# A fused linear-attention and gated-MLP kernel: decays by row transfers, and other orders, banks and holds

## The chip, the cores and the metric

The kernel runs on one core of one Trainium2 chip. The metric is device time in microseconds (us) of one execution; lower is better. The kernel before took 194.99 us, the median of three runs (193.37 to 195.72). The profile was taken in one further execution of 193.01 us, of which 191.3 us are the span from the first to the last instruction.

## What is computed

Attention with a decaying state over 4 batches, 8 heads, 768 steps, head size 48; then a gated feed-forward net (FFN) over the 3072 tokens, 384 wide, 1536 hidden:

```python
f = 1.0 / (1.0 + np.exp(-f_logit))
for t in range(S):
    state = f[:, :, t, :, None] * state + np.einsum('bhd,bhe->bhde', k[:, :, t], v[:, :, t])
    y[:, :, t] = np.einsum('bhd,bhde->bhe', q[:, :, t], state)
...
gate = np.maximum(x @ w_gate, 0.0)
val = x @ w_val
return (gate * val @ w_out).astype(np.float32)
```

## The kernel before, in words

Time is cut into six chunks of 128 steps. A *position* w = 4c + b (c from 0 to 5, b from 0 to 3) is one chunk of one batch; two positions make a *unit*. The first four units (positions 0 to 7, UNITS = 4) hold two chunks of one batch each, read as 96-float rows in which even and odd steps lie side by side; from position 8 on, a position is chunk c of batch b.

For each position the *front* (function `front`) turns f into negative log decays on ScalarE (ACT): `ef` (line 484, Exp) and `ln` (line 487). TensorE (PE) sums them over time with a triangular matrix: `cum` (lines 505 and 509 for the first units, 514 and 517 after). Line 517 makes four 1-column matmuls more, the sums over the whole chunk. ACT then forms `ek` (line 528, the growing factor) and `eq` (line 530, the shrinking one) in the tile `expo`, and from the whole-chunk sums the chunk's decay `dc` (line 538 for the first units, 545 after). `hk` and `hq` (lines 552 on GpSimd, called POOL, and 553 on VectorE, called DVE) multiply k and q by them into `hats`. The hats are turned by PE and copied back for positions 0 to 7 (`tk`, `tq`, line 564; copies `ck`, `cq`, lines 568 and 569), and by a DMA transpose from position 8 on (`xh`, line 572). `v` (lines 582 to 584) is a copy of v in bf16.

The scores `s` (lines 596, 662) are masked by DVE (`m`, lines 604, 669) into `ptm`. `y` (757, 764, 768, 684) and `yi` (720) give the chunk's output, `kv` (784, 707) what the chunk adds to the state, and `st` (454), or `ss` and `sd` (458, 460), the new state, scaled by the chunk's decay. The output becomes `x` (line 609), the FFN's turned input `xT`.

The FFN takes four positions at a time: `g` and `u` (line 804, the gate and value projections, 12 column groups of 128 each), `r` (relu, lines 809 and 810), `p` (line 812, the product), `o` (line 825), `d` (the copy out, 831 and 832), `S` (the store, 835). For chunk 0 the first four groups are done in halves: g00.0 to g00.3 for positions 0 and 1, g02.0 to g02.3 for positions 2 and 3 (256 columns instead of 512).

Loads are `L` with f, k, q or v, the chunk and the first position, so Lk0.2 (k0.2 in short) loads k for positions 2 and 3, the second unit; a load is 384 KB. They are issued from SyncE's queue (SP) and from ACT's. Weights come in column slices from POOL's queue, wg0+2 being groups 0 and 1 of w_gate.

Every operation is declared once with its reads, writes and possible engines (the class `Plan`). The order on each engine is then written out by hand of a planner, as lists of operation numbers (`ORDER`, line 24), and so are the PSUM banks in the order in which PE opens them (`BANKS`). From these the program works out which semaphore each instruction waits on. In PE's list `~3512` stands for three filler matmuls of 512 columns on zeros, put ahead of the next operation. `HELD` makes one operation wait for another that it doesn't need: in the kernel before, Lq0.0 for a memset, wv2+2 for hk02, Lq1.0 for yi03, Lv1.2 for tq13, wv8+4 for g02.1, wo0+4 for r00.6.

## Time and profile before

| what | value |
|---|---|
| median of three runs | 194.99 us |
| profiled execution, its time | 193.01 us |
| its span | 191.3 us |
| instructions in it | 4793 |
| granted TensorE clock | 1.0 throughout |
| moved by DMA | 32.43 MB |
| DMA packets under 512 B | 103472 of 110278 |

In the lines of the profile, `L804` is line 804 of the kernel; `ps<-xT,wg` names the tile written and the tiles read; `x219` is a count; a duration is in microseconds where a start stands before it, and in nanoseconds where it is a mean. What stands in brackets, or behind a bar with an arrow, is the idle time of the engine just before, and what ended it. PE's ends are modelled, so neighbouring matmuls overlap in the list; start to start is exact. PEld is PE's loading of weights.

### The profile page before, as it was taken

Reading aid. Unit: us, or ns where it says so; the run is one execution under the profiler, and the core shown is the slowest. Engines: PE = TensorE matmul, PEld = TensorE weight load, DVE = VectorE, ACT = ScalarE, POOL = GpSimd, SP = SyncE. Lnnn points to the kernel's source line nnn. Section 1 sums busy time; section 2 is a strip of 40 time slices with the busy share of each in tenths; the row PEclk is TensorE's granted clock in tenths of the full one; section 3 lists DMA queues with packets and bytes.
Section 4 is the critical chain, followed back from the end, with each engine's and each line's share of the span. In section 5 each row is a group of like instructions: output and inputs, shape, how many; then the busy total and the mean of one; then the engine's idle time right before and its main releaser. Section 6 shows DMA issues by size and latency. Waiting matters only on the chain.

```text
span 191.3 us, 4793 instructions
## 1 busy us (share of the span) xinstructions
PE 180.6 (94%) x1977; PEld 108.4 (57%) x1996; DVE 137.4 (72%) x249; ACT 92.0 (48%) x200; POOL 59.2 (31%) x88
## 2 busy tenths in 40 slices
PE   7597999989899999999999999999999999999994
PEld 7364785455655556655555654556656554455562
DVE  4299877986758778669868779988688485655620
ACT  3969663264477546497654574372233132301112
POOL 5638531741036702047371610492600000000000
PEclk9999999999999999999999999999999999999999
DMA  6999999969999999989999999999763300000223
GB/s 163 318 296 216 159 209 264 161 123 251 225 221 206 240 201 246 235 191 200 197 182 215 245 175 175 243 251 178 98 151 108 99 4 0 3 0 0 109 98 126
DMA packets 110278, 32.43 MB, mean 170 GB/s; under 512 B 103472, under 2 KB 110000, under 8 KB 110256
## 3 DMA queue, kind: packets, MB, share of 16 engines
q1 hardware_dynamic: 88960, 25.04, 61.7%
q0 software_dynamic: 3744, 3.54, 12.2%
q10 hardware_dynamic: 17552, 3.54, 10.0%
q8 instruction: 16, 0.26, 0.6%
q14 instruction: 6, 0.05, 0.1%
HBM read 25.95 MB, written 4.72 MB: 160 GB/s over the span
## 4 chain that ended last, share of the span: by engine, by line
PE 85%; DVE 8%; DMA 3%; issue 2%; ACT 0%; DVEq 0%; ACTq 0%
PE ps L804 46%; PE ps L825 25%; DVE hats L553 4%; DMA q_in<-in_q_dram 3%; PE ps L596 2%; PE ps L757 2%; PE ps L564 2%; PE ps L514 1%; DVE gT L812 1%; PE ps L662 1%; PE ps L684 1%; PE ps L784 1%; DVE ptm L669 1%; PE ps L768 1%; PE ps L764 1%
## 5 line engine op out<-in xcount | busy, mean ns | idle before, releaser
L812 DVE TENSOR_TENSOR gT<-relu,ps 128x512 bf16<-128x512 bf16 (+1 forms) x76 | 47.7, 653 | 19.7 <-PE ps L804 17.5
L804 PE MATMUL ps<-xT,wv 128*128 128x512 bf16 (+1 forms) x220 | 53.6, 367 | 0.6 <-issue 0.2
L804 PE MATMUL ps<-xT,wg 128*128 128x512 bf16 (+1 forms) x219 | 52.6, 368 | 0.6
L825 PE MATMUL ps<-wo,gT 128*128 128x384 bf16 (+2 forms) x300 | 52.0, 320 | 0.0
L809 ACT ACTIVATE relu<-ps 128x512 bf16<-128x512 f32 (+1 forms) x42 | 23.9, 576 | 47.8 <-PE ps L804 24.2
L825 PEld LDWEIGHTS ps<-wo,gT 128*128 128x128 bf16 x300 | 27.7, 98 | 18.3
L804 PEld LDWEIGHTS ps<-xT,wg 128*128 128x128 bf16 x228 | 23.6, 108 | 20.5 <-issue 0.4
L804 PEld LDWEIGHTS ps<-xT,wv 128*128 128x128 bf16 x228 | 23.3, 108 | 18.3
L552 POOL TENSOR_TENSOR hats<-q_in,expo 128x384 bf16<-128x384 f32 x17 | 17.9, 1058 | 30.2 <-DMA q_in<-in_q_dram 12.2
L810 DVE TENSOR_SCALAR relu<-ps 128x512 bf16<-128x512 f32 (+1 forms) x34 | 21.7, 654 | 5.4 <-PE ps L804 5.3
L552 POOL TENSOR_TENSOR hats<-k_in,expo 128x384 bf16<-128x384 f32 x17 | 17.7, 1050 | 21.2 <-ACT expo L528 14.9
L604 DVE TENSOR_TENSOR ptm<-ps,tri 128x512 bf16<-128x512 f32 x32 | 20.5, 684 | 5.1 <-PE ps L596 5.1
L831 ACT ACTIVATE osb<-ps 128x384 f32<-128x384 f32 (+1 forms) x16 | 7.6, 484 | 25.0 <-PE ps L825 22.2
L528 ACT ACTIVATE expo<-ps 128x384 f32<-128x384 f32 x24 | 11.7, 496 | 6.1 <-DVE hats L553 2.6
L530 ACT ACTIVATE expo<-ps 128x384 f32<-128x384 f32 x24 | 11.8, 492 | 2.0 <-PE ps L517 1.9
L460 POOL TENSOR_TENSOR st<-ssum,dec 128x384 bf16<-128x384 f32 x10 | 8.6, 864 | 10.0 <-DVE ssum L458 10.0
L669 DVE TENSOR_TENSOR ptm<-ps,tmask 128x512 bf16<-128x512 f32 x16 | 10.0, 678 | 2.1 <-PE ps L662 2.1
L484 ACT ACTIVATE f_in<-f_in 128x768 f32<-128x768 f32 x12 | 10.1, 840 | 2.8 <-DMA f_in<-in_f_logit_dram 2.8
L458 DVE TENSOR_TENSOR ssum<-ps,st 128x384 f32<-128x384 f32 x16 | 8.8, 550 | 2.7 <-PE ps L784 2.5
L553 DVE TENSOR_TENSOR hats<-q_in,expo 128x384 bf16<-128x384 f32 x7 | 8.2, 1167 | 3.4 <-DMA q_in<-in_q_dram 3.4
L487 ACT ACTIVATE bneg<-f_in 128x768 bf16<-128x768 f32 x12 | 10.1, 841 | 1.0 <-ACT osb L831 0.8
L564 PE MATMUL ps<-ident,hats 128*128 128x128 bf16 x64 | 5.5, 220 | 4.0 <-DVE hats L553 3.0
(78 smaller groups left out, 159.2 us busy)
## 6 DMA issues: line engine op xcount, KB each, us to landing
v_in<-in_v_dram SPq DMA_DIRECT2D x12, 384.0 KB, 5.5
out_dram<-osb SPq DMA_DIRECT2D x23, 192.0 KB, 2.3
k_in<-in_k_dram SPq DMA_DIRECT2D x10, 384.0 KB, 7.1
q_in<-in_q_dram SPq DMA_DIRECT2D x9, 384.0 KB, 5.8
f_in<-in_f_logit_dram SPq DMA_DIRECT2D x8, 384.0 KB, 4.8
f_in<-in_f_logit_dram ACTq DMA_DIRECT2D x4, 384.0 KB, 6.6
q_in<-in_q_dram ACTq DMA_DIRECT2D x3, 384.0 KB, 5.6
wv<-in_moe_w_val_dram POOLq DMA_DIRECT2D x2, 384.0 KB, 6.7
```

The costliest lines, as they stand in the source:

```text
L484: add(f"ef{c}{b0}", by("ACT", lambda: sc.activation(raw, raw, AF.Exp, scale=-1.0), act_(n)), keys, keys, key=P)
L528: add(f"ek{c}{b}", by("ACT", lambda: sc.activation(ex[:, 1, :], bc.ap[:, 0:HD], AF.Exp, scale=1.0), act_(HD)), [bc], [f"expk{ei}"], key=P + 1)
L530: add(f"eq{c}{b}", by("ACT", lambda: sc.activation(ex[:, 0, :], bc.ap[:, 0:HD], AF.Exp, scale=-1.0), act_(HD)), [bc], [f"expq{ei}"], key=P ...
L552: return {**by("POOL", lambda: gp.tensor_tensor(o, i_, e_, ALU.mult), pool_(HD)), **by("DVE", lambda: ve.tensor_tensor(o, i_, e_, ALU.mult ...
L553: **by("DVE", lambda: ve.tensor_tensor(o, i_, e_, ALU.mult), dve_(HD))}
L604: add(f"m{c}{b}{j}", by("DVE", lambda b=b, j=j, mi=mi: ve.tensor_tensor(ptm[mi][:, j, :, :], s[b, j].ap[:, :].rearrange("p (n t) -> p n t" ...
L669: add(f"m{c}{b2[i]}{j}", by("DVE", lambda i=i, j=j, mask=mask: ve.tensor_tensor(ptm[mi[i]][:, j, :, :], s[j, i].ap[:, :].rearrange("p (n t ...
L804: z = te.matmul(bank.ap[:, 0:n], wt[:, kt, w_cols(j)], xT[xi][:, kt, n0:n1], start=(kt == 0), stop=(kt == NK - 1))
L809: add(f"r{c}{b0}.{j}", {**by("ACT", lambda: sc.activation(rdst, gate.ap[:, 0:n], AF.Relu), act_(n)), **by("DVE", lambda: ve.tensor_scalar_ ...
L810: **by("DVE", lambda: ve.tensor_scalar_max(rdst, gate.ap[:, 0:n], 0.0), dve_(n))}, [gate], [f"relu{ri}"], key=P)
L812: add(f"p{c}{b0}.{j}", by("DVE", lambda: ve.tensor_tensor(gT[gi][:, j, n0:n1], rdst, val.ap[:, 0:n], ALU.mult), dve_(n)), [val, f"relu{ri} ...
L825: z = te.matmul(o.ap[:, 0:e1 - e0], gT[gi][:, j, b * C:(b + 1) * C], wo[:, j, e0:e1], start=(j == 0), stop=(j == NJ - 1))
```

## The change

*Decays by rows.* For positions 8 to 19 the sums of line 517 and the exponentials of line 545 are left out. The decay of a whole chunk is the last row of `eq`, so it is taken from there: partition 127 of `expq` is spread over 48 partitions of the tile `dec`, by two small DMAs for each pair of positions (`xd`; six steps of two DMAs, each of 48 pieces of 32 bytes). So that eight floats that belong together lie side by side, `eq` writes its result with a step of 64 bytes in these positions, and `hq` reads it so. `dec` changes its layout to match.

*Buffers.* `expo` becomes `expk` with 2 buffers and `expq` with 4 (2 pairs), in place of 3 of both. `zeros` shrinks from 512 to 128 columns (wide fillers read it repeatedly); `tlow` is laid over a sum buffer. `FOLD` (4) stands where `UNITS` (4) stood in `place`, and loads from position 8 on go through `place`.

*Orders, banks and holds.* All five lists and all banks are new. The opening filler is 12 matmuls of 512 columns, not 60 of 100. SP begins f0.0, q0.0, f0.2, k0.0, f1.0, k0.2, q0.2, f1.2, k1.0, v0.0, v0.2, q1.2, k1.2, q1.0, v1.2, f2.2 (before: f0.0, f0.2, k0.0, v0.0, k0.2, v0.2, q0.2, f1.2, f1.0, q1.2, q1.0, k1.0, k1.2, v1.2, v1.0, f2.0, with q0.0 on ACT). POOL takes wv2+2 first of all weights. PE's list up to the first FFN matmul, g00.0, now holds the cums of positions 4 to 7 too. Holds: Lv0.2 for eq03, S11 for eq42, Lv2.0 for hk21.

```diff
-NB, NE, NH, NQ, NM, NV, NA, NN, NS, NX, NG, NR, NO = 3, 3, 6, 6, 5, 6, 3, 4, 2, 2, 2, 4, 3
+NB, NE, NH, NQ, NM, NV, NA, NN, NS, NX, NG, NR, NO = 3, 2, 6, 6, 5, 6, 3, 4, 2, 2, 2, 4, 3
+FOLD = 4
+ROW_DECAYS = set(range(8, 20))
+NEQ = 2
...
-        45, ~60100, 74, 85, ~3512, 82, ~3512, 90, 80, 92, 121, ~1512, 95, 110, 101, 126, ~4512, 116, ~2512, 100, 128,
+        45, ~12512, 74, 85, ~6512, 110, ~1512, 80, 121, ~2512, 92, 82, 90, ~3512, 230, 95, 118, 116, ~2512, 128,
...
-    48: 10, 57: 114, 60: 140, 67: 284, 69: 164, 70: 185,
+    55: 123, 357: 694, 371: 389,
...
-    expo = sb("expo", [128, NE, 2, HD], F32)
+    expk, expq = sb("expk", [128, NE, HD], F32), sb("expq", [128, NEQ, 2, HD], F32)
...
-    decs = sb("dec", [128, NA, B, NP, 2], F32)
+    decs = sb("dec", [128, NA, 2, B, NP], F32)
...
-            if c < NC - 1:
+            if ch < NC - 1 and not rows:
                 for p in range(NP):
                     x = te.matmul(bc.ap[:, HD + p:HD + p + 1], bn[:, 2 * p:2 * p + 2, :].rearrange("p h d -> p (h d)"), ones[:, :])
...
+        ex = (expq[:, eqi, :, :].rearrange("q x h -> q (x h)").rearrange("q (d j x p) -> q x p j d", d=D, x=2, j=2)[:, b % 2, :, :, :] if rows
+              else expq[:, eqi, b % 2, :].rearrange("q (p j d) -> q p j d", p=NP, j=2),
+              expk[:, ei, :].rearrange("q (p j d) -> q p j d", p=NP, j=2))
...
+            def decay_rows(eng):
+                for j in range(2):
+                    at, to = expq[C - 1:C, eqi, 0, 2 * NP * j:2 * NP * j + 1], decs[64 * j:64 * j + D, ai, j, b0, 0:1]
+                    x = eng.dma_start(bass.AP(tensor=to.tensor, offset=to.offset, ap=[list(to.ap[0]), [1, 2 * NP]]),
+                                      bass.AP(tensor=at.tensor, offset=at.offset, ap=[list(at.ap[0]), [4 * NP, D], [1, 2 * NP]]))
+                    if j == 0:
+                        x.then_inc(xd.sem, 16)
+                return x
...
```

## The prediction

> **What bounds the kernel now.** I read the page first, then busy time by stage, then the chain of work in order of time, then the start instruction by instruction.

> ```profile
> PE 180.6 (94%) x1977; PEld 108.4 (57%) x1996; DVE 137.4 (72%) x249; ACT 92.0 (48%) x200; POOL 59.2 (31%) x88
> PE 85%; DVE 8%; DMA 3%; issue 2%; ACT 0%; DVEq 0%; ACTq 0%
> ```

> The tensor engine is busy for 94% of the span and makes 85% of the chain that ends last. A gain must therefore be PE work that goes, a shorter start, or a gap closed in the middle. Busy time by stage says where such gaps are (columns: stretch, length, then PE, PEld, DVE, ACT and POOL, each with its instructions, the granted clock, the DMA share, GB/s):

> ```profile
> 0.00:19.84 19.84, 14.55 (x300) 10.70 (x303) 13.39 (x42) 14.41 (x27) 11.49 (x34) 1.00 1.01 243
> 19.84:35.00 15.16, 14.99 (x190) 10.17 (x183) 12.34 (x24) 7.56 (x20) 5.84 (x8) 1.00 1.15 210
> 35.00:55.00 20.00, 18.40 (x348) 11.46 (x349) 16.26 (x28) 9.54 (x19) 5.78 (x9) 1.00 1.07 197
> 55.00:120.00 65.00, 64.68 (x658) 36.89 (x662) 49.86 (x85) 41.41 (x98) 25.27 (x27) 1.00 1.12 209
> 120.00:180.00 60.00, 59.38 (x436) 33.65 (x443) 42.75 (x68) 17.16 (x35) 10.85 (x13) 1.00 0.44 92
> 180.00:191.30 11.30, 8.61 (x63) 5.51 (x61) 2.83 (x5) 1.87 (x5) 0.00 (x0) 1.00 0.35 127
> ```

> Length less PE's busy time gives its idle time: 5.29 us before 19.84 (and part of its busy time there is filler on zeros), 1.60 us between 35 and 55, 0.94 us in the 125 us after that, 2.69 us at the end. From 55 to 180 us there is next to nothing to win by order, only something to lose. The start and the stretch from 35 to 55 decide.

> ```profile
> 4.16 0.84 ACT L484 ACTIVATE f_in<-f_in 128x768 f32<-128x768 f32 x1 [2.07 <-DMA f_in<-in_f_logit_dram]
> 7.10 0.87 ACT L528 ACTIVATE expo<-ps 128x384 f32<-128x384 f32 x2
> 8.06 0.99 POOL L552 TENSOR_TENSOR hats<-k_in,expo 128x384 bf16<-128x384 f32 x1 [1.38 <-ACT expo L528]
> 8.19 1.28 DVE L553 TENSOR_TENSOR hats<-q_in,expo 128x384 bf16<-128x384 f32 x1 [3.35 <-DMA q_in<-in_q_dram]
> 10.30 0.55 DVE L553 TENSOR_TENSOR hats<-q_in,expo 128x384 bf16<-128x384 f32 x1
> 17.14 0.60 ACT L609 ACTIVATE xT<-ps 128x384 bf16<-128x384 f32 x1
> 19.13 0.59 DVE L609 CAST xT<-ps 128x384 bf16<-128x384 f32 x1
> 19.84 0.50 PE L804 MATMUL ps<-xT,wg 128*128 128x256 bf16 x3
> ```

> The first FFN matmul starts at 19.84, when DVE has written the second xT block (x01, 19.13 to 19.72). The start hangs on DVE: it began hq00 at 8.19, when the q load had landed, and needed 11.53 us from there to the end of x01, almost without a gap.

> **The change, part by part.** *Decays by rows.* For positions w = 8 to 19 the four 1-column matmuls behind each cum go, and two small ACT exponentials with them; six steps of two small DMAs each come instead.

> ```profile
> 55.66 0.16 PE ps L514
> 55.82 0.08 PE ps L517 x4
> 55.90 2.61 PE ps L804 x12
> 61.47 0.70 ACT L545 ACTIVATE dec<-ps 64x4 f32<-64x4 f32 x4
> 71.51 0.83 POOL L460 TENSOR_TENSOR st<-ssum,dec 128x384 bf16<-128x384 f32 x1 [5.73 <-DVE ssum L458]
> L413 ACTq DMA_DIRECT2D f_in<-in_f_logit_dram x4: 374/374/1402, 46.8 to 75.6; - x4
> qkT<-hats SPq DMA_TRANSPOSE x16, 3.3
> DMA to landing us min/median/max: 2.7/3.3/8.2
> ```

> On a full PE the four cost 0.08 us (55.82 to 55.90). There are 12 such groups, all in PE's full stretch: 12 x 0.08 = **-0.96**. ACT loses 24 exponentials of 0.175 us (four in 0.70), 4.2 us, and gets the 12 DMA issues, since all six xd stand on its list. No row has so small a transfer there; a full load costs 0.37 us to issue and 1.40 at worst, so 4.4 to 16.8 us in all, and I take 4.4, because the median of that row is its minimum. ACT is free for 23.6 of the 65 us after 55, which hides either end; without that cover the surplus (0.2 to 12.6) would delay relus and so PE. The landing is bounded by the nearest transfers between SBUF tiles, the transposes of hats: 2.7 to 8.2 us, median 3.3 (the last two rows). A state update that needs a decay of chunk 2 ran at 71.51 and had been waiting for DVE's sum, ten microseconds after that chunk's last decays (61.47). So even 8.2 us is hidden, and I take 0; with the slack gone, the update on POOL would hold up the hats queued behind it, and these the next scores.

> *Strided expq.* In these positions eq writes, and hq reads, one float in every 64 bytes. No row shows such a step. The nearest are ACT's copy to x00 with a 4-byte step, 0.60 us, and a plain ek, 0.44: from 0 to +0.5 us for each of 12 eq and 12 hq, and I take the middle. That is 3 us on ACT and up to 3 on POOL, which is busy for 25.3 of the 65 us after 55: hidden, 0 on the path.

> *Expk from 3 buffers to 2, expq to 4.* An ek now waits for the hk two positions back instead of three. The price lies between 0 (ACT is 48% busy) and one hat on POOL, 1.05 us by a row below, for each time that it bites; I take 0, since in the new lists each hk stands shortly behind its ek. *Zeros, tlow, the layout of dec, FOLD*: shorter memsets and the same values (FOLD equals UNITS, so place and load do what they did): 0.

> *The new start.* SP now issues f0.0, q0.0 (from ACT's list, 0.37 us less there), f0.2, k0.0, f1.0, k0.2, q0.2, f1.2, k1.0, v0.0, and holds v0.2 until eq03; v1.0 moves to ACT (0.37 more), behind a relu; wv2+2 goes first on POOL, with no hold.

> ```profile
> GB/s 0 0 77 188 326 324 320 297 314 324 326 323 312 215 276 326 325 334 309 317 267 256 275 105 156 83 122 153 171 175 195 180 184 186 197 217 195 255 301 308
> L553 DVE TENSOR_TENSOR hats<-q_in,expo 128x384 bf16<-128x384 f32 x3 | 3.8, 1269 | 3.4 <-DMA q_in<-in_q_dram 3.4
> L568 DVE COPY qkT<-ps 128x512 bf16<-128x512 bf16 x5 | 1.9, 419 | 0.1
> L583 DVE CAST vpad<-v_in 128x384 bf16<-128x384 f32 x1 | 0.3, 350 | 0.0
> L353 DVE TENSOR_TENSOR tmask<-tmask,tlow 128x128 bf16<-128x128 bf16 x2 | 0.4, 218 | 0.0
> ```

> The first row has slices of 0.75 us from 0 to 30: a load of 0.393 MB takes 1.21 us at 324 GB/s. f0.2 is now the third load: 4.16 + 2 x 1.21 = 6.58. ACT then does ef02 (0.84), dc00 (two of 0.175), ln02 (0.84, as ef02), ek00 and eq00 (0.435 each, by the pair at 7.10). eq00 is done at 9.5, and hq00 starts 1.3 us later than now although its q is there. DVE's list from hq00 to x01 has two copies (0.84) and v00 (0.35) more and one add (0.22) less: +0.97. Of the 11.53 us about 2.2 was slowing of hats while POOL worked (three at 1.27 against the 0.55 at 10.30). x01 ends at 9.5 + 11.53 + 0.97 = 22.0 with as much slowing, at 19.8 with none, at about 21.2 with two slowed hats; hk00 on POOL beside hq00, and hk03 beside hq03, make two likely. ACT sets a floor: from 6.58 to x00 it has six f passes (5.04), fourteen ek and eq (6.1), four decay pairs (1.4) and two copies (1.2), so x00 is done near 20.6 at best, overlaps allowed. v0.0, now tenth, with 0.6 MB of weights ahead, lands near 17; DVE comes to its copy near 18. First FFN matmul: 21.3, bounds 20.6 and 22.6 (all five slowed, and DVE waiting for eq03 once), against 19.84.

> How a hat is slowed shows at 8.06: POOL's hat ran to 9.05, and DVE's, started at 8.19, ended at 9.47, 0.42 after it. [...]

> By its first FFN matmul PE has also done work that now comes later:

> ```profile
> 20.34 0.33 PE ps L505 x2
> 20.67 0.18 PE ps L509 x8
> 28.12 0.22 PE ps L564 x4
> 50.13 0.79 PE ps L707 x32
> 33.31 2.09 DVE hats L553
> 38.85 1.28 DVE hats L553
> k_in<-in_k_dram SPq DMA_DIRECT2D x4, 384.0 KB, 7.1
> wg<-in_moe_w_gate_dram POOLq DMA_DIRECT2D x2, 384.0 KB, 9.0
> L552 POOL TENSOR_TENSOR hats<-k_in,expo 128x384 bf16<-128x384 f32 x17 | 17.7, 1050 | 21.2 <-ACT expo L528 14.9
> L435 POOL DMA_DIRECT2D wg<-in_moe_w_gate_dram x4 | 3.3, 822 | 0.0
> ```

> Two cums of 0.51, two of 0.16 and a transpose of 0.22, less kv02 (0.39, half of the 0.79), which moves behind: 1.2 us. Net: 1.46 - 1.2, about **+0.3**, bounds -0.4 and +1.6.

> *The weights.* wv4+4, wv8+4 and wg8+4 now stand on POOL behind hats that need q1.2, k1.2 and q1.0, and these loads stand on SP behind the held v0.2. eq03 is done near 14 (ten more ACT steps after eq00, some 4.3 us); k1.2, third after it, is issued at 16.4 and lands 7.1 later, at 23.5. POOL then has three hats (1.05) and two weight issues (0.82) ahead of wg8+4: issued at 28.3, landed 9.0 later, 37.3. PE, for its part, has from its first FFN matmul to g00.11 sixteen half-width groups (0.33, half of a quarter of the 2.61), ten full ones (0.65), seven transposes (0.22) and six score, output and state steps (an estimate, at kv02's 0.39): 15.7 us, so it wants wg8+4 at 37.0. I take **+0.4**, bounds 0 and +5.

> *The gap at 35 to 55.* The chain shows two DVE hats (2.09 and 1.28 us) holding transposes of units 2 and 3. All eight of those units' hats are now POOL's, and their transposes stand among the first FFN groups. Of the 1.60 us idle I take **-1.2**, bounds 0 and -1.6; next late would be the weights. *Middle, end, the other banks and holds*: the same instructions in another order, 0.94 us of idle to begin with: 0, and +2 (a second gap like that at 35) as the price of a bad place.

> Sum: -0.96 + 0.3 + 0.4 - 1.2 = -1.5 us. The profiled execution took 193.01 (span 191.3), so 191.5; the median of the three runs, 194.99, lies 1.98 above it, and on that footing I forecast **193.5 us**.

> **The rivals.** *The start works as ordered.* DVE's hats are unslowed, the FFN starts at 20.6, weights are in time and the gap goes: -0.96 - 0.4 - 1.6 = -3.0, so 192.0. For it: the hat at 10.30 needed only 0.55. Against: POOL's list is fuller in those microseconds. *The weights come late (slower).* If k1.2 lands 4 us after 23.5, everything behind it on POOL slips as much, and PE stands at g00.11 with the columns listed behind it: +4.4 in place of +0.4, so 197.5; with the bounds of the start, 199. It decides once k1.2 lands after 25. For it: loads and weight slices share the queues then, and the rate fell to 83 to 200 GB/s from 17 to 27 us. Against: a hold frees the queues too. *Nothing on the path changes:* the start takes what the matmuls give, and the gap stays because DVE is late elsewhere: -0.96 + 1.0, so 195.0.

> **How the numbers follow.** Forecast 0.48, start as ordered 0.18, weights late 0.21, nothing 0.13. The likeliest one's own range is 192 to 195.5; the neighbours and their bounds make 191.0 to 198.0. About what a measurement of this kernel can tell from no change is 2%, here 191.1 and 198.9. Below the first lies a third of the second case and a tenth of the forecast's: 0.11. Above the last lie half of the late weights and part of the +2 in the middle: 0.14. Between them: 0.75.

> **What would show it.** In the changed profile: no 1-column matmuls after 53 us, and 0.16 us for a cum there; hq00 near 9.5 and the first FFN matmul near 21.3; PE idle under 0.6 us from 35 to 55; wg8+4 landing near 37 with PE waiting for it under 1 us; state updates of chunk 2 released by DVE's sum, not by a DMA. The forecast is wrong if hq00 starts as early as 8.2, if the first FFN matmul comes after 23, or if PE idles over 1.5 us between 55 and 180.

## The result and the profile after

The kernel after took 195.84 us, the median of 20 runs (194.31 to 198.09), against 193.98 us for the kernel before (20 runs, 191.78 to 197.13): ratio 1.011, 95% interval 1.0085 to 1.0135. It is slower by about 1%, where 0.8% faster had been forecast for the profiled execution (191.5 of 193.01). Its own profiled execution took 195.80 us, span 194.0 us; 2.7 us of span are to be explained. Ratios, here and below, leave out executions that took over 1.5% longer than the fastest of their kernel; medians do not.

The page of after, first its busy times, then the engines' shares of the chain that ends last:

```profile
PE 184.5 (95%) x1904; PEld 106.3 (55%) x1904; DVE 135.3 (70%) x250; ACT 89.7 (46%) x174; POOL 62.8 (32%) x89
PE 77%; DMA 8%; ACT 4%; POOL 4%; DVE 2%; issue 2%; SPq 1%; DVEq 0%
```

PE lost instructions and gained busy time: 1904 matmuls stand against 1996 before (the page of before lists 1977, but 1996 weight loads; 19 of its matmuls are missing from the record). 48 of the 92 are the 1-column matmuls, the rest opening fillers. Busy time by stage, columns as in the prediction, shows where:

```profile
0.00:19.84 19.84, 16.34 (x142) 8.62 (x143) 11.64 (x40) 13.78 (x28) 10.81 (x31) 0.92 1.03 244
19.84:35.00 15.16, 14.95 (x341) 10.84 (x339) 12.32 (x27) 9.57 (x23) 12.23 (x15) 0.99 1.16 236
35.00:55.00 20.00, 17.50 (x286) 9.81 (x285) 14.47 (x25) 8.45 (x15) 3.63 (x5) 1.00 1.08 199
55.00:120.00 65.00, 65.00 (x616) 36.47 (x615) 51.88 (x86) 34.25 (x62) 29.39 (x31) 1.00 0.95 193
120.00:180.00 60.00, 59.36 (x452) 33.65 (x450) 40.46 (x69) 20.33 (x42) 6.68 (x7) 1.00 0.48 108
180.00:194.00 14.00, 11.32 (x77) 6.95 (x74) 4.49 (x8) 3.32 (x7) 0.00 (x0) 1.00 0.21 75
```

Two stages differ. The granted clock in the start is 0.92, not 1.00; and PE idles 2.50 us between 35 and 55, not 1.60. By these rows nothing was lost from 55 us to the end, as predicted. DVE's and PE's rows in the start, in order of time (line 592 is the hats' 553 of before, 464 the state of 454, 648 the x copy of 609, 844 the FFN's 804):

```profile
9.53 1.64 DVE L592 TENSOR_TENSOR hats<-q_in,expq 128x384 bf16<-128x384 f32 x2 [3.07 <-ACT expq L550]
18.05 0.61 DVE L622 CAST vpad<-v_in 128x384 bf16<-128x384 f32 x2
21.00 0.56 DVE L464 TENSOR_TENSOR st<-ps,dec 128x384 bf16<-128x384 f32 x1 [1.74 <-PE ps L746]
22.27 0.58 DVE L648 CAST xT<-ps 128x384 bf16<-128x384 f32 x1
22.91 0.50 PE L844 MATMUL ps<-xT,wg 128*128 128x256 bf16 x3
```

hq00 starts at 9.53, but the first FFN matmul at 22.91, 3.07 us later than before. On the way DVE, the engine that was to set the start, waits 1.74 us for PE (kv00, line 746). What PE did then, by stretches of 3.41 us (length, PE busy, granted clock, DMA share, GB/s):

```profile
9.76:13.18 3.42, 2.49 (x23) 1.00 1.16 317
13.18:16.59 3.41, 2.12 (x52) 1.00 1.04 269
16.59:20.00 3.41, 3.41 (x27) 0.50 1.26 217
20.00:23.41 3.41, 3.36 (x133) 1.00 1.06 274
```

For exactly one stretch, 16.59 to 20.00, PE runs at half clock, with kv00 queued behind a cum, transposes and fillers. After that, these are PE's only idle times above 0.15 us before the end, each in the bracket of its row:

```profile
31.20 1.46 PE L844 MATMUL ps<-xT,wg 128*128 128x512 bf16 x6 [0.16 <-DMA wg<-in_moe_w_gate_dram]
35.32 2.11 PE L844 MATMUL ps<-xT,wv 128*128 128x512 bf16 x9 [0.23 <-DMA wv<-in_moe_w_val_dram]
48.78 0.35 PE L759 MATMUL ps<-qkT,st 128*32 128x128 bf16 x11 [2.26 <-issue]
139.32 0.81 PE L844 MATMUL ps<-xT,wg 128*128 128x512 bf16 x3 [0.22 <-DVE ssum L468]
161.94 1.46 PE L844 MATMUL ps<-xT,wg 128*128 128x512 bf16 x6 [0.28 <-issue]
```

The weights cost 0.39 us. The gap that DVE's hats made is gone (0.81 us at 40.78 before; its row names gT, which stood behind the hat of 38.85 on DVE). In its place stand 2.26 us in the middle of a unit of small matmuls (line 759 is yi, 720 before); "issue" says that PE waited for nothing that the profile shows. The kernel before has the same kind of stall, 0.55 us, in the same group of units:

```profile
40.78 0.62 PE L564 MATMUL ps<-ident,hats 128*128 128x128 bf16 x8 [0.81 <-DVE gT L812]
52.05 0.85 PE L684 MATMUL ps<-ptm,vpad 64*32 64x128 bf16 x74 [0.55 <-issue]
120.69 1.24 PE L804 MATMUL ps<-xT,wv 128*128 128x512 bf16 x5 [0.17 <-issue]
```

The account: first FFN matmul +3.07; the idle times listed behind it 3.15 in place of 1.53, +1.62; so PE's work and shorter gaps behind it must be 1.99 less (3.07 + 1.62 - 1.99 = 2.70). 0.96 of that are the 1-column matmuls. The other 1.03 would be the work that now stands ahead; it is what is left over, not a measurement (the view of busy times has PE's work 0.95 less in all, but lacks at least nine of before's matmuls there).

### The profile page after: what moved, and what is told of

Its sections match the earlier page's. It is cut to its first block, busy times and chain, and to the rows that moved or that the text cites. A ratio compares the mean times of both kernels' runs of the same rounds, so it can differ in the third digit from the quotient of the medians.

```text
span 194.0 us, 4609 instructions
## 1 busy us (share of the span) xinstructions
PE 184.5 (95%) x1904; PEld 106.3 (55%) x1904; DVE 135.3 (70%) x250; ACT 89.7 (46%) x174; POOL 62.8 (32%) x89
## 4 chain that ended last, share of the span: by engine, by line
PE 77%; DMA 8%; ACT 4%; POOL 4%; DVE 2%; issue 2%; SPq 1%; DVEq 0%
PE ps L844 44%; PE ps L865 21%; DMA wv<-in_moe_w_val_dram 4%; POOL hats L591 2%; DMA f_in<-in_f_logit_dram 2%; PE ps L635 2%; DMA out_dram<-osb 2%; PE ps L797 2%; PE ps L526 1%; ACT expk L548 1%; DVE hats L592 1%; PE ps L824 1%; PE ps L931 1%; PE ps L808 1%; ACT bneg L498 1%
## 5 line engine op out<-in xcount | busy, mean ns | idle before, releaser
L844 PE MATMUL ps<-xT,wg 128*128 128x512 bf16 (+1 forms) x228 | 54.2, 368 | 0.7 <-issue 0.3
L865 PE MATMUL ps<-wo,gT 128*128 128x384 bf16 (+2 forms) x300 | 53.6, 320 | 0.0
L591 POOL TENSOR_TENSOR hats<-k_in,expk 128x384 bf16<-128x384 f32 x18 | 18.7, 1044 | 55.3 <-ACT expk L548 47.1
L844 PEld LDWEIGHTS ps<-xT,wg 128*128 128x128 bf16 x228 | 23.6, 108 | 20.8 <-DVE ssum L468 1.0
L643 DVE TENSOR_TENSOR ptm<-ps,tri 128x512 bf16<-128x512 f32 x32 | 20.3, 684 | 3.8 <-PE ps L635 3.8
L591 POOL TENSOR_TENSOR hats<-q_in,expq 128x384 bf16<-128x384 f32 x15 | 17.3, 1167 | 11.6 <-DMA q_in<-in_q_dram 11.5
L871 ACT ACTIVATE osb<-ps 128x384 f32<-128x384 f32 (+2 forms) x17 | 7.9, 471 | 27.7 <-PE ps L865 27.3
L550 ACT ACTIVATE expq<-ps 128x384 f32<-128x384 f32 x24 | 15.4, 663 | 8.0 <-PE ps L526 7.2
L548 ACT ACTIVATE expk<-ps 128x384 f32<-128x384 f32 x24 | 11.7, 496 | 12.8 <-PE ps L526 10.9
L470 POOL TENSOR_TENSOR st<-ssum,dec 128x384 bf16<-128x384 f32 x13 | 11.2, 866 | 15.6 <-DVE ssum L468 15.5
L931 PE MATMUL ps<-zeros 128*128 128x512 bf16 x29 | 10.7, 504 | 0.5 <-DVE ptm L708 0.5
L592 DVE TENSOR_TENSOR hats<-q_in,expq 128x384 bf16<-128x384 f32 x9 | 7.0, 789 | 5.4 <-ACT expq L550 3.4
## 6 DMA issues: line engine op xcount, KB each, us to landing
f_in<-in_f_logit_dram SPq DMA_DIRECT2D x12, 384.0 KB, 6.1
out_dram<-osb SPq DMA_DIRECT2D x23, 192.0 KB, 2.6
q_in<-in_q_dram SPq DMA_DIRECT2D x11, 384.0 KB, 5.7
k_in<-in_k_dram SPq DMA_DIRECT2D x9, 384.0 KB, 5.6
v_in<-in_v_dram SPq DMA_DIRECT2D x7, 384.0 KB, 6.7
v_in<-in_v_dram ACTq DMA_DIRECT2D x5, 384.0 KB, 4.4
k_in<-in_k_dram ACTq DMA_DIRECT2D x3, 384.0 KB, 4.4
wg<-in_moe_w_gate_dram POOLq DMA_DIRECT2D x2, 384.0 KB, 8.9
```

Of the source, the lines that this page charges most:

```text
L470: emit = {e: (lambda g=g: g.tensor_tensor(t4(s_new), t4(tmp), rate, ALU.mult)) for e, g in (("POOL", gp), ("DVE", ve))}
L548: add(f"ek{c}{b}", by("ACT", lambda: sc.activation(ex[1], parts(bc.ap[:, 0:HD]), AF.Exp, scale=1.0), act_(HD)), [bc], [f"expk{ei}"], key=P ...
L550: add(f"eq{c}{b}", by("ACT", lambda: sc.activation(ex[0], parts(bc.ap[:, 0:HD]), AF.Exp, scale=-1.0), act_(HD)), [bc], [f"expq{eqi}_{b % 2 ...
L591: return {**by("POOL", lambda: gp.tensor_tensor(o, i_, e_, ALU.mult), pool_(HD)), **by("DVE", lambda: ve.tensor_tensor(o, i_, e_, ALU.mult ...
L643: add(f"m{c}{b}{j}", by("DVE", lambda b=b, j=j, mi=mi: ve.tensor_tensor(ptm[mi][:, j, :, :], s[b, j].ap[:, :].rearrange("p (n t) -> p n t" ...
L844: z = te.matmul(bank.ap[:, 0:n], wt[:, kt, w_cols(j)], xT[xi][:, kt, n0:n1], start=(kt == 0), stop=(kt == NK - 1))
```

## The experiments

Theories: **A**, the new start costs, by its order or by its clock; **B**, the row decays cost, by their DMA issues on ACT or by the stepped expq; **F**, PE ran out of instructions at 46 us. Ratios are to the kernel before on the same chip. Orders are written by the operations' names.

The recorded expectations have letters of their own. A in rows_only and order_only: the loss is in the new orders. C: the halved clock in the start; D: DVE and ACT (in f_second, ACT's late second f pass). E in spread, and F from shift on: PE's instruction supply; F in spread is the opposite, a wait for a result. G, R and L are about the row transfers, U about a stall that belongs to its unit.

**rows_only: row decays in the orders of before.**

```diff
 ACT (orders of before)
-  dc21, ef22, eq20, ln22 ... dc20    # dc of positions 8 to 19
+  ef22, eq20, xd20, ln22             # xd behind the pair's later eq
```

> The orders, banks and holds of the kernel before, with decays by rows put in: each xd stands on ACT right behind the later of its two eq, expk keeps 3 buffers. Theory A (the row decays are a small gain, the loss is in the new order): PE loses the 1-column matmuls, 12 x 0.08 = 0.96 us, the first FFN matmul stays near 19.8, and the time is 0.5 to 1 us under the kernel before. Theory B (the row decays cost: strided expq, small transfers): slower than before by 1 us or more, with PE or POOL waiting for expq or for dec.

Measured: 197.25 us (195.94 to 199.07), ratio 1.0186 (1.0137 to 1.0234). ACT, then PE, around its worst place:

```profile
56.65 2.02 ACTq L567 DMA_DIRECT2D dec<-expq  x2
58.71 0.84 ACT L496 ACTIVATE bneg<-f_in 128x768 bf16<-128x768 f32 x1 [2.10 <-issue]
```

The two issues held ACT for 2.02 us, the logarithm behind them came late, PE waited 3.00 us for it (at 59.70) and then ran one stretch of 3.41 us at half clock. So row decays can cost, where their issue stands ahead of something due.

**rows_late: the same, five of the six xd two to four steps later (xd22 stays).**

```diff
-  eq20, xd20, ln22, v20, r10.3, ek20
+  eq20, ln22, v20, r10.3, ek20, xd20
```

> Before's orders with the row decays, as in rows_only, but each pair of row transfers is issued on ACT one to three steps later, behind the next logarithm, so that no logarithm stands behind it. If rows cost only where their issue holds up ACT (theory R), the PE idles of rows_only between 55 and 106 us (3.00, 0.51, 0.63, 0.90 us) fall to under 0.6 us each, and the 48 one-column matmuls that go (0.96 us) are won: 0.3 to 1.0 us below the kernel before beside it. If the longer expq and the later state update cost wherever the transfers stand (theory L), it stays 1 us or more above before, with idles on PE that end by expq, hats or the state update.

Measured: 192.98 us (191.64 to 194.91) beside 193.9 of before, ratio 0.9973 (0.9939 to 1.0006), all 12 runs at full clock. The 3.00 us are gone; the longest idle between 55 and 106 us is 0.32. The whole loss of rows_only was the place of the issue. Row decays by themselves win about 0.5 us by this ratio, and by its interval between 1.2 us and nothing; with 0.96 us of matmuls removed that is in keeping.

**order_only: the orders of after, decays as before.**

```diff
-ROW_DECAYS = set(range(8, 20))
+ROW_DECAYS = set()
```

> The orders, banks and holds of the changed kernel, with the decays as before (four 1-column matmuls and two small exponentials for each of positions 8 to 19, each pair of exponentials right behind its ek and eq). Theory A: the first FFN matmul near 22 to 23 as in the changed kernel, and the time 0.5 to 1 us above the changed kernel, so 2.5 to 3 us above the kernel before. Theory B: 1 us or more below the changed kernel, about at the kernel before.

Measured: 198.54 us (195.75 to 199.46), ratio 1.0186 (1.0119 to 1.0253). First FFN matmul at 21.79, with the same lists for the start as after, at full clock. The loss is in the orders; PE's row at 48.91, with the same 11 matmuls left as in after:

```profile
34.74 2.11 PE L844 MATMUL ps<-xT,wv 128*128 128x512 bf16 x9 [0.57 <-DMA wv<-in_moe_w_val_dram]
48.91 0.35 PE L759 MATMUL ps<-qkT,st 128*32 128x128 bf16 x11 [3.09 <-issue]
```

A stretch at half clock follows, from 49.22.

**more_fill: after, ten more wide fillers in the start.**

```diff
-        45, ~12512, 74, 85, ~6512, 110, ~1512, 80, 121, ~2512, 92, 82, 90, ~3512, 230, 95, 118, 116, ~2512, 128,
+        45, ~12512, 74, 85, ~6512, 110, ~4512, 80, 121, ~2512, 92, 82, 90, ~6512, 230, 95, ~2512, 118, ~2512, 116,
```

> The changed kernel with ten more filler matmuls of 512 columns at places in the start where PE stood idle (three ahead of tk00, three ahead of cum10, two ahead of tq02, two ahead of tk02). Theory C (in the changed kernel PE idles enough between 10 and 16 us that its clock is halved for some 3.4 us, which delays kv00 and with it the first FFN matmul): granted clock 1.00 in every stretch, first FFN matmul near 21.3 in place of 22.9, and the time 1 to 1.5 us under those runs of the changed kernel whose clock was 0.991, about 194.9. Rival D (DVE and ACT set the start whatever PE's clock): first FFN matmul after 22.5, time as the changed kernel or above by the fillers.

Measured: 195.15 us (192.36 to 197.41), ratio 1.0019 (0.9974 to 1.0065). The spread has two heaps: 5 runs with a mean clock of 1.0 average 193.1, 7 with 0.991 average 196.1, and five of these 7 are not in the ratio; the median of all is 1.0% above that of before (193.19 beside it). The profiled run is of the first kind, 192.36 us, 0.65 below the profiled run of before: first FFN matmul at 20.85, the stall shorter and nine matmuls earlier:

```profile
24.06 0.38 PE L603 MATMUL ps<-ident,hats 128*128 128x128 bf16 x4 [0.41 <-POOL hats L591]
33.58 2.11 PE L844 MATMUL ps<-xT,wv 128*128 128x512 bf16 x9 [0.24 <-DMA wv<-in_moe_w_val_dram]
46.30 0.46 PE L759 MATMUL ps<-qkT,st 128*32 128x128 bf16 x20 [1.66 <-issue]
```

So at full clock the start is 2.06 us earlier than in after. That the fillers did it isn't shown. The profiled runs of order_only, spread and xd_on_sp have after's lists for the start without these fillers, kept the full clock there too, and began the FFN at 21.79, 21.75 and 20.87; stall_fill, with the fillers, at 21.74. What is shown is theory A by its clock: DVE waits 1.74 us for kv00 in after and 0.17 in each of the three, and against them the half clock cost after's start 1.1 to 2.0 us. Of the four executions with these lists and no added fillers, after's is the only one that had it in the start.

**f_second: f0.2 ahead of q0.0 on SP.**

```diff
-        46, 48, 50, 47, 58,
+        46, 50, 48, 47, 58,
```

> The changed kernel with the loads of f0.2 and q0.0 exchanged on SP, so that f0.2 is second. Theory D (ACT's second f pass, 0.7 us late in the changed kernel, sets eq00, hq00 and so the start): ef02 at 5.9 in place of 6.64, hq00 near 8.9, the first FFN matmul 0.7 us earlier and the time 0.5 to 0.7 us lower. Theory C (PE's halved clock sets it): first FFN matmul earlier by under 0.3 us, or it moves with the clock alone.

Measured: 195.9 us (194.88 to 198.11), ratio 1.0145 (1.0093 to 1.0197). First FFN matmul at 21.42, 1.49 earlier than in after, the start at full clock; but the stall is 2.54 us, and the half clock comes behind it, from 48.39. What the start won is lost there. hq00 came at 8.95, as theory D had it; but against order_only, at full clock too, the start is only 0.37 earlier, less than such starts differ among themselves (20.87 to 21.79), so most of the 1.49 is the clock.

**spread and spread_fill: big groups between the units of small matmuls**, without and with the fillers of more_fill.

```diff
-  g00.10, u00.11, o02.0, kv12, y10, y12, yi13, yi11, o03.0
+  g00.10, y10, u00.11, o02.0, kv12, y12, o03.0, yi13, yi11
```

> The changed kernel with the block of small matmuls ahead of chunk 0's output spread out on PE: y10, u00.11, o02.0, kv12, y12, o03.0, yi13, yi11 in place of u00.11, o02.0, kv12, y10, y12, yi13, yi11, o03.0. Theory E (PE runs out of instructions when some 340 of them come within 2.1 us; the 2.26 us of idle in the middle of yi11, with no wait, is that): the idle time there falls under 0.5 us and the time by 1.5 to 2.5 us against the changed kernel, more in runs in which the clock fell after it. Rival F (yi11 waits for a result, from DVE or a DMA): idle time of about 2 us stays, now ahead of yi13 or yi11, and the time stays.

> The changed kernel with both: the small matmuls spread, and the ten fillers more in the start. Theories C and E together: first FFN matmul near 20.9, no stretch with a granted clock below 1.00 before 180 us, no idle time over 0.5 us in yi11, and 191 to 192.5 us, so 1 to 2 us under the kernel before. If only one of them holds, 193.5 to 195.

Measured: 195.44 us (194.33 to 196.27), ratio 1.0107 (1.0075 to 1.0139), and 194.62 us (193.85 to 197.33), ratio 1.008 (1.0049 to 1.011). All 15 runs were at full clock. The chief idle rows of PE in spread:

```profile
34.78 1.89 PE L844 MATMUL ps<-xT,wv 128*128 128x512 bf16 x8 [0.74 <-ACT qkT L608]
43.62 0.73 PE L723 MATMUL ps<-ptm,vpad 64*32 64x128 bf16 x64 [1.27 <-ACT relu L849]
49.47 0.40 PE L759 MATMUL ps<-qkT,st 128*32 128x128 bf16 x14 [1.50 <-issue]
```

The stall shrank only to 1.50 us, where under 0.5 had been expected, and the moved y10 now waits 1.27 us for ACT. What spreading won went into new waits. spread_fill kept a stall of 1.36 us and missed its 191 to 192.5; in its profiled run, the longest of the nine (197.33), the FFN began at 23.10, where 20.9 had been expected.

**rows_sp and xd_on_sp: the row transfers issued from SP**, in the orders of before and of after.

```diff
-  ACT ... xd20 ...
+  SP  ... xd20, xh20 ...
```

> The orders, banks and holds of the kernel before with decays by rows, and the two small DMAs issued from SP just ahead of the transposes of the same positions, not from ACT (expk with 3 buffers). Theory G (rows by themselves are cheap; on ACT each pair of issues takes 1 to 2 us and holds up the ln behind it, and with it a cum): no 3 us wait of PE for bneg near 57 us, and 0 to 1 us under the kernel before. Rival B (strided expq or the transfers themselves cost): still 1 us or more above the kernel before, with PE waiting for ACT in chunks 2 to 4.

> The changed kernel with the small decay DMAs issued from SP ahead of the transposes, not from ACT. If ACT's time on the issues costs the changed kernel anything, 0.5 us or more faster; if they are hidden there, as was predicted, within 0.4 us of it, and the idle times of PE after 55 us as before (under 0.7 us in all).

Measured: 204.68 us, ratio 1.0537 (1.0485 to 1.0589), and 204.29 us, ratio 1.0551 (1.051 to 1.0593). Both expectations missed by far. SP's queue, ACT and PE in xd_on_sp, where the loss is:

```profile
89.97 2.00 SPq L876 DMA_DIRECT2D out_dram<-osb  x1
93.36 1.22 SPq L570 DMA_DIRECT2D dec<-expq  x2
95.83 0.81 ACT L551 ACTIVATE expq<-ps 128x384 f32<-128x384 f32 x1 [9.09 <-DMA dec<-expq]
97.39 0.50 PE L527 MATMUL ps<-bneg,tri 128*128 128x384 bf16 x1 [5.14 <-ACT expk L549]
```

On SP the row transfer stands behind an output store and a transposition; ACT's next eq needs the expq buffer that this transfer reads, so ACT stood still for 9.09 us and PE for 5.14, and two stretches at half clock followed. A transfer that frees a buffer belongs to a queue in which nothing slower stands ahead of it.

**shift: many small fillers where more_fill had few wide ones.**

```diff
-  110, ~4512, 80 ... 90, ~6512, 230, 95, ~2512, 118, ~2512, 116
+  110, ~12128, 80 ... 90, ~12128, 230, 95, ~8128, 118, ~8128, 116
```

> After with 40 more start fillers of 128 columns where more_fill had 10 more of 512: about the same filler time, 30 matmuls more. If the stall at 46 us is PE's instruction supply (theory F), it stands at a fixed number of instructions: as the 10 matmuls of more_fill moved it 9 matmuls earlier (from 11 to 20 state matmuls of the unit left), it stands here about 30 earlier still, with about 24 state matmuls and 26 of L723 left, and lasts 0.8 to 1.7 us. If it belongs to the unit or its operands (theory U), it stays with 11 to 20 state matmuls left at 1.6 to 2.3 us. Time between 193 and 195.5 by either.

The batches of 12 stand in place of all wide fillers at their two spots, so the kernel has 1940 matmuls, 26 more than more_fill. Measured: 192.19, 195.44, 196.29 and 197.33 us, too wide to say anything on the time. The place is the point; PE's row:

```profile
47.32 0.35 PE L723 MATMUL ps<-ptm,vpad 64*32 64x128 bf16 x22 [2.72 <-issue]
```

22 of this line and 24 of line 759 are left, 46 in place of 20: the stall moved by 26 matmuls, as many as were put in, into another unit with other operands. It stands at a count of instructions. Its length was expected at 0.8 to 1.7 and was 2.72.

**stall_fill: more_fill, six more wide fillers among the small matmuls.**

```diff
-  kv12, y10, y12, yi13, yi11
+  kv12, ~3512, y10, ~3512, y12, yi13, yi11
```

> more_fill with six more fillers of 512 columns (1.28 us) in the dense stretch of small matmuls, three ahead of y10 and three ahead of y12. Theory F: PE works through them while the next instructions are fetched, the stall shrinks from 1.66 to 0.2 to 0.7 us, runs at full clock stay at more_fill's 193.1 within 0.4 us, and few runs have a halved clock: median 193.0 to 194.0. Theory U or any fixed wait: the stall stays and the fillers come on top, 194.2 or more at full clock.

Measured: 194.86 us (193.68 to 200.2), ratio 1.0068 (1.0028 to 1.0108).

```profile
48.30 0.23 PE L723 MATMUL ps<-ptm,vpad 64*32 64x128 bf16 x2 [1.09 <-issue]
```

26 are left in place of 20, six again. The clock held (11 of 12 runs at full clock, 5 of 12 in more_fill), but the stall shrank by only 0.57 us for 1.28 us of filler. The median expected, 193.0 to 194.0, was missed, and the 11 runs average 195.0, where 193.1 within 0.4 had been expected. In the profiled run (196.5 us) 1.63 us of PE's idle time stand elsewhere, ahead of 146.96, for a transposition of hats; the profiled run of more_fill has no such wait.

**no_fill: the kernel before without its 13 wide fillers** (3 + 3 + 1 + 4 + 2; the expectation counts 15).

```diff
-        45, ~60100, 74, 85, ~3512, 82, ~3512, 90, 80, 92, 121, ~1512, 95, 110, 101, 126, ~4512, 116, ~2512, 100, 128,
+        45, ~60100, 74, 85, 82, 90, 80, 92, 121, 95, 110, 101, 126, 116, 100, 128,
```

> The kernel before without its 15 fillers of 512 columns in the start (the 60 at the very beginning stay). Theory C (a start with too much idle PE loses the clock): first FFN matmul within 0.4 us of 19.84 when the clock is full, but a stretch of 3.4 us at half clock in most runs, each about 1.2 to 1.7 us longer: median 0.7 to 1.7 us above before. If fillers buy nothing, the same time as before within 0.4 us. By theory F its small stall in y10 (0.55 us, with 74 of L684 left) moves 15 matmuls later, to about 59 left.

Measured: 194.35 us (192.65 to 195.79), ratio 1.0028 (0.9992 to 1.0064). PE by stretches:

```profile
7.81:11.23 3.42, 1.56 (x18) 1.00 1.25 287
11.23:14.64 3.41, 3.21 (x62) 0.50 1.17 317
14.64:18.05 3.41, 3.02 (x89) 0.50 1.00 240
```

The clock fell in every run, in the profiled one for three stretches, and the first FFN matmul came at 19.88, 0.04 later than before: in this order PE waits for DVE anyway (1.85 us ahead of 9.52 and 1.17 ahead of 17.64 in before), and slow work fits into the waits. So half a clock has no fixed price: it was 1.1 to 2.0 us in the start of after, where DVE waits for PE, and 0.04 here. That expectation failed on the time (0.28% by the ratio, not clear of nothing). The stall of 0.55 us, expected with about 59 matmuls left, did not show at all; the next paragraphs say why.

**What ends the stall.** The DMA view lists queues of their own for instructions. The larger, q8, has 15 packets in after, 0.25 MB in all, so 16 KB each; with PE's 3869 recorded instructions (matmuls, weight loads, semaphores) that would be some 64 bytes for each, by estimate. No view names the engine it serves; it is taken to be PE's because of the times below. The trace has the time of each packet. Beside the stalls (us; "left" is the count of small matmuls that the unit group still has to do):

```
kernel       left  PE stops  PE resumes  stall  packet     resume - packet's end
after          11   46.52     48.78      2.26   46.56-47.44      1.34
f_second       11   45.12     47.66      2.54   45.31-46.23      1.43
order_only     11   45.82     48.91      3.09   46.50-47.46      1.45
xd_on_sp       11   45.05     47.47      2.42   45.12-46.08      1.39
spread         14   47.97     49.47      1.50   47.07-48.00      1.47
more_fill      20   44.64     46.30      1.66   43.92-44.97      1.33
spread_fill    23   49.40     50.76      1.36   48.42-49.37      1.39
stall_fill     26   47.21     48.30      1.09   46.04-47.00      1.30
shift          46   44.60     47.32      2.72   44.99-45.95      1.37
```

With stalls between 1.09 and 3.09 us, PE goes on 1.30 to 1.47 us after such a packet has ended, nine times of nine (the short stalls in the orders of before, 0.55 in before and 0.35 in rows_late, end 1.68 and 1.61 us after theirs).

The place is sharper still when all of PE's recorded instructions are counted from the start. The stall stands behind number 1473 in all seven stalled kernels whose record is complete: after, f_second, order_only, more_fill, shift, stall_fill and rows_late, in two orders and at five places of the group (in after 722 matmuls, 723 weight loads and 28 others). In before, spread, spread_fill and xd_on_sp it stands behind 1469 or 1470, and their records lack 18 or 19 matmuls. Where PE comes to this number late enough, nothing stops it: no_fill passes it at 51.80, 1.49 us after the packet's end (50.31), rows_only at 50.32, 1.43 after (48.89). This settles F: at that number PE had used up its instructions, and the length of the stall is how late the packet was. The group kv12, y10, y12, yi13, yi11 is 168 matmuls with a weight load each, and after did 157 of them in 2.07 us (44.45 to 46.52). In before the packet had ended 1.14 us ahead of PE's stop (50.36, 51.50), in after 0.92 us behind it (47.44, 46.52). What sets the start of the packet stays open: where the group stands together, it begins 1.9 to 2.8 us behind the group's first matmul in six kernels of seven, and 1.2 us behind it in more_fill, at different counts of instructions; so it also isn't shown why stall_fill won so little.

## Why the prediction failed, step by step

Two steps failed: the gap at 35 to 55 us, in all nine kernels of the table above, and the new start, which PE's half clock delayed in the profiled execution. In order of the sum:

- **1-column matmuls, -0.96:** right. A cum of chunk 2 is followed at once, 0.16 us later, by the next group, and no such matmul is left.
- **The new start, +0.3:** about +2.0 (3.07 later, less some 1.0 of work moved ahead by the account above; 1.2 had been taken). The first half of the step held: hq00 at 9.53 for 9.5, two slowed hats of five on DVE (hq00 1.08 us, hq02 1.25, the others 0.55 to 0.64), the v copies at 18.05 for "near 18". x01 ended at 22.85; without DVE's 1.74 us of waiting for kv00 that is 21.1, where 21.2 was forecast. What failed is that the sum followed DVE and ACT alone and took PE as the receiver. PE was itself in DVE's path by kv00, and ran a stretch at half clock, which the forecast had no term for. The same lists at full clock gave 20.87 to 21.79 (xd_on_sp, spread, order_only), where 21.3 had been forecast. Of the 20 runs of after, the 8 with a mean clock of 0.999 or more average 194.95, the 10 with 0.990 or 0.991 average 196.19, 1.24 us more. Where the half clock lay is recorded for the profiled run alone (in f_second, order_only and shift it lay behind the stall), so the 1.24 are not the start's price. And the 8 are still 1.0 us above the median of before: the half clock is not the whole loss. (Two slips in the working move nothing: ACT's floor adds up to 20.3, not 20.6, and eight ACT steps, not ten, lie between eq00 and eq03.)
- **The weights, +0.4:** 0.39, but by luck. The term was built from wg8+4, to land at 37.3 for a PE that wants it at 37.0. It landed at 40.3 (issued at 31.18, 9.2 us), PE came to it at 40.47, and nothing waited; the 0.39 are waits for wg4+4 and wv4+4 (31.20, 35.32). The rival that made the weights hold up PE by 4 us did not come.
- **The gap at 35 to 55, -1.2:** measured +0.90 (2.26 less 0.55 and 0.81). DVE's hats went, as forecast; "next late would be the weights" was wrong. Next late were PE's own instructions: 2.26 in place of 0.55 us, and 1.09 to 3.09 in the eight other kernels of the table. The row of before with "issue" in its bracket was the warning, and the prediction passed over it.
- **The row transfers:** hidden, as forecast, but dearer. The rows of the tile dec in after (the issue's ns, least, median and most; then issue to landing in us):

```profile
L569 ACTq DMA_DIRECT2D dec<-expq x12: 508/588/914, 60.3 to 126.9; - x12
DMA to landing us min/median/max: 1.7/3.1/4.0
```

12 x 0.59 = 7.1 us of ACT against 4.4 taken, inside the bounds; rows_only shows that it is no harmless term. They land within 4.0 us. The view of waits has POOL's state updates wait for DVE's sum and for no transfer (us in all, times, longest), both as forecast:

```profile
POOL st L470 <- DVE ssum L468: 15.5, 4, 8.1
```

- **Stepped expq:** an eq with the step takes 0.82 to 0.87 us, one without 0.48 to 0.53: about +0.33, near the middle of the range. A hat that reads it takes 1.19 to 1.34 in place of 1.00 on POOL, 0.92 and 1.02 in place of 0.55 on DVE. All hidden.
- **Middle and end, 0:** nearly; 0.64 us idle from 55 to 180 by the stages, while the listed idle times behind 55 are 0.50 in place of 0.17.

Of the 4.2 us between the forecast for this execution (-1.5) and what came (+2.7), about 1.7 lie in the start and 2.1 in the stall. The footing for the median was high as well: before lies 0.97, not 1.98, above its profiled execution when 20 runs are taken. The range held the time, but the slower rival had named the wrong mechanism, and none of the three signs that were to show the forecast wrong was reached, the start missing its 23 by 0.09 us.

Of the versions tried, rows_late is the best: no slower than before, and by the two intervals (up to 1.0006, and from 1.0085) faster than after. It keeps the row decays and drops the new orders.

## What to carry to other kernels

When an order moves PE work ahead of the point that other engines wait for, follow PE as a worker with a clock of its own: keep its idle share low there (the half-clock periods listed below came behind stretches in which PE was busy for 0.20 to 2.12 us of 3.41), or put nothing behind the slow stretch that another engine needs (in after DVE waited 1.74 us for kv00). Read an idle time that ends by "issue" in a run of tiny matmuls as a possible shortage of instructions (1.09 to 3.09 us in the table above): look for the instruction packet beside it, and expect the wait to grow when a new order brings PE to that place earlier (0.55 us at 51.50 in before, 2.26 us at 46.52 in after). A small DMA costs its queue's order more than its bytes (1.5 KB each here; two issues held ACT for 2.02 us in rows_only, and PE waited 3.00 us): place its issue where nothing due stands behind it, and not behind anything slow if it frees a buffer (9.09 us of waiting on ACT in xd_on_sp).

## What the hardware showed that was not expected

*Instructions.* What is taken to be PE's instructions comes in packets of 16 KB, 15 in after and 16 in before, each 0.88 to 1.59 us long there, and one that came late held PE up for as long as 3.09 us (order_only).
